# First key products by full-width weights: a re-planned start of an attention and state-space kernel

## The chip, the cores and the metric

The kernel runs on one core of a Trainium2 chip. The metric is the device time of one execution in microseconds (us); smaller is better. A core has five engines with queues of their own: PE (TensorE, matrix products; its weight loads are shown as PEld), DVE (VectorE), ACT (ScalarE), POOL (GpSimd) and SP (SyncE, which here only issues DMA transfers). They wait for one another by semaphores.

## The reference

Two blocks of 2048 positions and 640 channels, whose results are put side by side. A is a state-space layer: a complex recurrence along the positions, run between two products with dense matrices. B is attention with 32 query heads of 20 channels which share one key head and one value head.

```
def _A_ref(x, ...):
    Lam_bar = exp(exp(log_dt) * Lam);  B_bar = ((Lam_bar - 1) / Lam)[:, None] * B
    Bu = einsum("bld,pd->blp", x, B_bar)
    h[t] = Lam_bar * h[t-1] + Bu[t]              # for all 2048 t
    return 2 * real(einsum("blp,dp->bld", h, C)) + x * Dskip

def _B_ref(x, wq, wk, wv, wo):
    q = (x @ wq) as 32 heads of 20;  k = x @ wk;  v = x @ wv
    p = softmax(q @ k^T * 20 ** -0.5)            # for each head, 2048 x 2048
    return (p @ v, heads side by side) @ wo
return concatenate([a, b], axis=-1)              # bfloat16
```

## The kernel before

**Tiles.** Scores are made transposed: 128 keys by 512 queries of one head are one tile, a matrix product of 32 rows, and there are 2048 tiles. ACT takes the exponential of two or three tiles that lie side by side in PSUM with one instruction (L1481, 1024 or 1536 columns). The other tiles (a share of 0.29) go to DVE, which turns scores into bfloat16 bits by integer arithmetic (L863, from PSUM into BIG); each such tile is copied three times with integer offsets, by POOL in pairs (L1796) or by DVE. PE multiplies all of them with the values (PR with VP, BIG with VS) and adds them up in one bank. The state-space layer and the projections ride along between score products as background tasks.

**A planned order.** The program is not written in the order in which it runs. `Build` submits operations with an engine, a duration, dependencies and a priority; `Schedule.run` plays them through against its own durations, always starting the ready operation with the lowest priority number on a free engine; `planned` does this for 32 seeds (L550) and keeps the plan whose replays end first. The order of each engine's queue and every wait come from that plan. Constants such as the landing times `LANDS` and `XB`, the duration given to an operation, and its `prio` therefore move the order, also long after the place where they stand.

**The start.** Ahead of the first exponential lies this:

- SP loads blocks 0 and 1 of x (512 positions each) as they are, then a part of the query weights, and then issues three transposing loads (L711) for block 2, the first three column chunks of block 3 and its last two (`XB`). ACT's queue loads the key weights into `wkr` (L706).
- PE turns blocks 0 and 1 by products with the identity (`turn`, four products for each of 5 chunks of 128 channels); the turned chunk is copied out of PSUM by DVE (L1121, "d") or ACT (L1124, "a"), as `TURNED` says for each block.
- `kv(tb)` makes the keys of block tb. Each key column is wanted four times, on the four strips of 32 rows. Blocks below `QUAD_KEYS` get this by four products with 32 columns of `wkr`, which run side by side (`four`); the others by one product with 128 columns of `wks`, a copy of `wkr` with every column group four times (L1035, on POOL). Block 3 is done in two halves of 256 columns in the order of `KEY_STEPS`, since its last two chunks land last.
- DVE finds the largest magnitude of the keys (L1152, L1178), `KT` is evicted by DVE or ACT as `KEYS` says (L1158 or L1161), a bound is made from the maximum (`bound`, L1180) and added to the first query row with four products (L1280), DVE evicts it as QT (L1286), and the first scores follow.
- At the same time the scalars of the state-space layer (`ssm_scalars`) run through PE, DVE and ACT, up to tables of sines (`fr` on DVE and POOL, L2135 on ACT).
- While PE has nothing else to do, `warm_source` gives it products with zeros (MB from PR) to keep it busy; later ones with VZ.

**What the edit touches**: `warm_source` (L912 to L927), the loads of L1031 to L1038, the constants of L1070 to L1074, the products and the reduction in `kv` (L1137 to L1155) and `KEY_STEPS` (L1247). In this kernel those that are read as lines of the profile are L726 (products made by `mm`), L1146 (key products with `wks`), L1263 (first query products), L1035 (the copy to `wks`) and L1202 (value products).

Of the kernel before, what the change touches and what calls it, by code (L numbers as in the profile page):

```python
# [11 lines left out]
ACT = mybir.ActivationFunctionType  # L12
ALU = mybir.AluOpType
AX = mybir.AxisListType
FP32 = mybir.dt.float32
# [441 lines left out]
S, D, NC, H, DH = 2048, 640, 5, 32, 20  # L457
# [8 lines left out]
class Build:  # L466
# [445 lines left out]
    def warm_source(self):  # L912

        if self.pv_first or self.s.t > 40000.0:
            return None
        p = self
        if self.started:
            if self.s.recent(3000.0) > self.WARM:
                return None
            fns = self.four(self.pvbank, [p.VZ[:]] * 4, p.KT[:, 0:512], True, True)  # L920
            return Op("pe", fns, self.mmt(512), prio=3.5, mode="C", load=512.0, reads=["VZ", "KT0"], writes=[self.pvbank.key],
                      deps=[self.c_op["VZ"], self.kt_op[0]])
        return Op("pe", [self.mm(self.pvbank.ap, p.PR[:, 0, 0:128], p.PR[:, 0, :], True, True)], 440.0 if self.s.t < 5000.0 else 250.0, prio=9,
                  load=512.0, deps=[self.zero_op], reads=["PR0"], writes=[self.pvbank.key], hook=self.warm_last)

    WARM = 4500.0
    V_AT, V_BY = (-97.5, -95.5), (22, 34)  # L927


# [89 lines left out]
    def loads(self):  # L1019
        p = self  # L1020
# [14 lines left out]
        self.wks_op = self.pool(lambda e: e.tensor_copy(spread, again), 800, deps=[self.wk_op], reads=["wkr"], writes=["wks"],  # L1035
                                prio=self.WKP, port=True)
        self.vec_op.append(vec[3]("sp"))
        self.wqa_op = L(wqd[:, :, 0:80], wqv[:, :, 0:80], 200000, "wqa", strided=True, writes=["wqa"], prio=0)  # L1038
        for tb, lo, hi, at in self.XB:
# [3 lines left out]
            for c in range(lo, hi):  # L1043
                self.xb_op[tb, c] = o
        self.wv_op = L(p.wvr[:], p.wv.rearrange("(c p) n -> p c n", p=128), 228000, "wv", strided=True,
                       writes=["wvr"])
# [5 lines left out]
                                prio=0.9, port=True)  # L1052
        for o, t in zip(self.vec_op + self.xn_op + [self.wk_op, self.wqa_op, self.wv_op, self.wq_op], self.LANDS):
            o.lands = t
# [4 lines left out]
                       writes=[f"xaT{tb}_{c}_{eo}" for tb in range(2) for c in range(NC)], gate=self.bound_made) for eo in range(2)]  # L1059
# [50 lines left out]
    def kv_steps(self):  # L1110
        p = self
# [19 lines left out]
        def kv(tb):  # L1131
            yield lambda: all((tb, c) in self.xb_op for c in range(NC)) and (tb < self.PLAIN or self.s.done([self.xb_op[tb, 0]])) \
                and any(x in self.early for x in self.free_banks)
            bank = self.take(self.early, self.KEY_BANKS)
            prev = None
            parts = 1 if tb < 3 else 2
            n = 512 // parts  # L1137
            steps = [(x, c) for x in range(parts) for c in range(NC)] if tb < 3 else self.KEY_STEPS
            for x, c in steps:
                at = 512 * tb + n * x  # L1140
                if tb < self.QUAD_KEYS:
                    prev = self.pe(self.four(bank, [p.wkr[:, c, :]] * 4, p.xbT[:, c, at:at + 512], c == 0, c == NC - 1), self.mmt(512),
                                   mode="C", prio=self.KP[tb], deps=[self.xb_op[tb, c], self.wk_op] + bank.last, prev=prev,
                                   reads=[f"xbT{tb}_{c}", "wkr"], writes=[bank.key])
                else:
                    prev = self.pe([lambda e, x=x, c=c, at=at: e.matmul(bank.cols(n * x, n * x + n), lhsT=p.wks[:, 128 * c:128 * c + 128],  # L1146
                                                                        rhs=p.xbT[:, c, at:at + n], start=c == 0, stop=c == NC - 1,
                                                                        skip_group_check=True)],
                                   self.mmt(n), prio=self.KP[tb], deps=[self.xb_op[tb, c], self.wks_op] + bank.last, prev=prev,
                                   mode="F", load=float(n), reads=[f"xbT{tb}_{c}", "wks"], writes=[bank.key])  # L1150
                if c == NC - 1:
                    red = self.dve(lambda e, src=bank.cols(n * x, n * x + n), to=p.mab[:, tb + x:tb + x + 1]: e.tensor_reduce(  # L1152
                        out=to, in_=src, axis=AX.X, op=ALU.max, apply_absolute_value=True), 115 + 1.05 * n, deps=[prev], reads=[bank.key],
                        writes=[f"mab{tb + x}"], prio=0.31 if x == parts - 1 else 0.315)
                    self.red_op[tb + x] = red  # L1155
            dst, src = p.KT[:, 512 * tb:512 * tb + 512], bank.ap
            if self.KEYS[tb] == "a":
                kt = self.act(lambda e: e.activation(dst, src, ACT.Identity, bias=p.lift[:, 2:3], scale=ALPHA * UNIT), 600,  # L1158
                              deps=[red, self.lift_op], reads=[bank.key, "lift"], writes=[f"KT{tb}"], prio=0.34)
            else:  # L1160
                kt = self.dve(self.ts(dst, src, ALPHA * UNIT, p.lift[:, 2:3], ALU.mult, ALU.add), 640,  # L1161
                              deps=[red, self.lift_op], reads=[bank.key, "lift"], writes=[f"KT{tb}"], prio=0.44)
            self.kt_op[tb] = kt
            yield lambda: kt.start is not None
            bank.last = [kt]
            self.give(bank)
            if tb < 2:
                yield lambda: any(x in self.early for x in self.free_banks)
                yield from self.v_task(tb, self.take(self.early, self.KEY_BANKS))
            else:  # L1170
                self.tasks.append((self.V_AT[tb - 2], 0, lambda: self.started, lambda bank: self.v_task(tb, bank)))
                self.tasks.sort(key=lambda t: t[0])
# [1404 lines left out]
```

## Time and profile before

| | before |
|---|---|
| runs, us | 708.70, 708.71, 708.75 |
| median, us | 708.71 |
| the profiled execution, device time, us | 708.9 |
| its span, first to last instruction, us | 707.2 |
| granted TensorE clock, mean | 1.000 |
| first exponential starts, us | 19.38 |
| last exponential ends, us | 698.83 |
| DMA traffic, mean over the span | 49 GB/s |

Busy time is the time in which at least one instruction of an engine ran. A row of the costliest groups reads: line, engine, operation, output from input, shapes, count, then busy us, mean ns of one, and the engine's idle time just before them with what ended it. A row of a timeline reads: start, length, engine, line, operation; neighbours of one kind are merged, and the bracket is idle time before the first. A row of the chain of waits in order of time reads: start, length, engine, line. The span's first 20 us are shown in more detail by the views quoted below than by the page, whose slices are 17.7 us long.

### The profile page before, as it was taken

The page shows a single profiled execution, that of the slowest core. Times are in us where ns is not written, and L with a number is a line of the kernel's source. Part 1 is how long each engine was busy: PE and PEld are TensorE (multiplying, and loading weights), DVE is VectorE, ACT ScalarE, POOL GpSimd, SP SyncE. Part 2 cuts the span into 40 slices and gives each one's busy share as a digit, 9 for nine tenths or more (in the row PEclk, how much of TensorE's full clock was granted, in tenths as well). Part 3 has the DMA queues.
Part 4 walks back from the last instruction along what each step waited for, and adds up shares of the span by engine and source line. Part 5 has one row for each costly group of instructions (what it writes and reads, how often), then busy time and mean ns, then how long its engine had stood idle before and what let it go on. Part 6 is the DMA issues. An engine that isn't in the chain of part 4 may idle for free.

```text
span 707.2 us, 26738 instructions
## 1 busy us (share of the span) xinstructions
PE 689.4 (97%) x11235; PEld 247.7 (35%) x11235; DVE 621.2 (88%) x1193; ACT 690.3 (98%) x698; POOL 462.4 (65%) x784
## 2 busy tenths in 40 slices
PE   8999999999999999999999999999999999999997
PEld 4322233443333533334333333333333333343323
DVE  7899999999899788878889998899999997978794
ACT  6999999999999999999999999999999999999996
POOL 4266574046787566955857847766767768778880
PEclk9999999999999999999999999999999999999999
DMA  9577741021120010103001010121000011100001
GB/s 224 145 173 164 160 112 52 25 48 31 26 50 13 18 26 27 38 20 66 18 18 29 19 28 26 43 57 19 13 14 20 13 22 35 39 20 20 21 15 40
DMA packets 77590, 34.44 MB, mean 49 GB/s; under 512 B 58351, under 2 KB 77471, under 8 KB 77471
## 3 DMA queue, kind: packets, MB, share of 16 engines
q1 hardware_dynamic: 76506, 32.44, 19.0%
q8 instruction: 90, 1.47, 0.9%
q10 hardware_dynamic: 964, 0.29, 0.2%
q14 instruction: 30, 0.24, 0.1%
HBM read 11.53 MB, written 9.75 MB: 30 GB/s over the span
## 4 chain that ended last, share of the span: by engine, by line
ACT 56%; PE 36%; DVE 4%; SPq 1%; DMA 1%; issue 1%; POOL 1%; DVEq 0%; POOLq 0%
ACT PR L1481 56%; PE MB L726 13%; PE MB L796 10%; PE SC L726 8%; PE MB L806 4%; DVE BIG L863 2%; SPq L711 1%; PE SC L796 1%; DMA BIG<-in_B_x_dram 1%; POOL BIG L1796 1%; PE SC L722 0%; DVE prod L858 0%; DVE BIG L1303 0%; SPq L707 0%; DVE stg L2048 0%
## 5 line engine op out<-in xcount | busy, mean ns | idle before, releaser
L1481 ACT ACTIVATE PR<-SC 128x1024 bf16<-128x1024 f32 (+1 forms) x677 | 676.7, 1190 | 4.3 <-PE SC L726 3.0
L1796 POOL INT64_ADD BIG<-BIG x748 | 449.3, 617 | 216.3 <-DVE BIG L863 102.7
L863 DVE TENSOR_SCALAR BIG<-SC 128x512 int16<-128x512 f32 x532 | 358.1, 686 | 62.7 <-PE SC L726 55.3
L726 PE MATMUL SC<-QT,KT 32*128 32x512 bf16 x2011 | 264.8, 384 | 7.6 <-ACT PR L1481 3.2
L726 PE MATMUL MB<-BIG,VS 128*32 128x512 bf16 x2276 | 256.8, 384 | 0.0
L726 PE MATMUL MB<-PR,VP 128*32 128x512 bf16 x1479 | 216.8, 384 | 0.0
L726 PEld LDWEIGHTS SC<-QT,KT 32*128 32x128 bf16 x2011 | 68.0, 90 | 177.3 <-ACT PR L1481 105.6
L726 PEld LDWEIGHTS MB<-BIG,VS 128*32 128x32 bf16 x2276 | 61.3, 94 | 65.5 <-issue 42.0
L726 PEld LDWEIGHTS MB<-PR,VP 128*32 128x32 bf16 x1479 | 52.6, 94 | 44.5 <-issue 31.8
L796 PE MATMUL MB<-CT,W 128*32 128x320 bf16 (+2 forms) x1008 | 53.2, 301 | 0.2
L863 DVE TENSOR_SCALAR BIG<-BIG 128x1024 int16<-128x1024 int16 (+1 forms) x110 | 42.0, 417 | 4.4 <-PE MB L726 4.2
L796 PE MATMUL MB<-CA,W 128*32 128x512 bf16 (+1 forms) x640 | 36.4, 302 | 0.9 <-issue 0.8
L806 PE MATMUL MB<-xaT,BT 32*128 32x256 bf16 x176 | 34.0, 272 | 1.3 <-ACT PR L1481 1.1
L796 PE MATMUL MB<-xaT,BA 128*32 128x256 bf16 x800 | 32.6, 275 | 0.0
L806 PE MATMUL MB<-diagD,xaT 32*128 32x128 bf16 x320 | 31.3, 217 | 0.0
L796 PEld LDWEIGHTS MB<-CT,W 128*32 128x32 bf16 x1008 | 23.2, 96 | 16.6 <-issue 7.4
L806 PEld LDWEIGHTS MB<-diagD,xaT 32*128 32x128 bf16 x320 | 17.7, 92 | 28.4 <-ACT PR L1481 17.3
L796 PE MATMUL MB<-xaT,BT 128*32 128x256 bf16 x624 | 26.3, 274 | 0.0
L858 DVE TENSOR_TENSOR prod<-MB,tab 128x1024 bf16<-128x1024 f32 x20 | 24.4, 1218 | 1.7 <-PE SC L726 1.0
L863 DVE TENSOR_SCALAR BIG<-MB 128x512 int16<-128x512 f32 x37 | 25.2, 680 | 0.2 <-PE MB L726 0.2
L2048 DVE CAST stg<-MB 128x512 bf16<-128x512 f32 x35 | 23.8, 679 | 1.2 <-PE MB L796 0.8
L796 PE MATMUL MB<-WO,OP 128*32 128x128 bf16 (+1 forms) x480 | 23.3, 301 | 0.2
(170 smaller groups left out, 467.9 us busy)
## 6 DMA issues: line engine op xcount, KB each, us to landing
out_dram<-stg SPq DMA_DIRECT2D x31, 128.0 KB, 1.9
qd<-BIG SPq DMA_DIRECT2D x20, 128.0 KB, 2.4
QT<-qd SPq DMA_DIRECT2D x28, 80.0 KB
OP<-pvsb SPq DMA_DIRECT2D x105, 20.0 KB
rdP<-recs SPq DMA_DIRECT2D x105, 20.0 KB
lbd<-BA SPq DMA_DIRECT2D x5, 320.0 KB, 2.8
CT<-in_B_x_dram SPq DMA_DIRECT2D x2, 640.0 KB, 5.3
BA<-in_A_B_re_dram SPq DMA_DIRECT2D x1, 800.0 KB, 7.0
```

The lines of the kernel that those rows point to most:

```text
L711: fns = [lambda e, o=o, i=i: e.dma_start_transpose(o, i) for o, i in pairs]
L726: return lambda e: e.matmul(out, lhsT=lhsT, rhs=rhs, start=start, stop=stop, **kw)
L796: x = e.matmul(out[32 * j:32 * j + 32], lhsT=lhsT[:, 32 * j:32 * j + 32], rhs=rhs, start=start, stop=r.end is tag, tile_position=(0, 32 * ...
L806: return lambda e: e.matmul(out, lhsT=lhsT[at], rhs=rhs[at], start=False, stop=r.end is tag, tile_position=(32 * row, 0), skip_group_check ...
L858: return lambda e: e.tensor_tensor(out, a, b, op)
L863: return lambda e: e.tensor_scalar(out, a, s1, s2, op0=op0, op1=op1)
L1481: ex = self.act(lambda e: e.activation(dst, t[:, 0:512 * n], ACT.Exp, scale=1.0 / UNIT), 0.8333 * 512 * n + 64, table="exp", deps=[op], re ...
L1796: op.fns.append(lambda e: e.int64_add(words(dst), words(src), add))
L2048: ev = self.dve(lambda e: e.tensor_copy(st, bank.ap), 645, deps=[prev], reads=[bank.key], writes=[key], prio=self.EV, gate=(lambda: last.e ...
```

## The change

The keys of block 0 are made like those of the other blocks, with the four-fold weights (`QUAD_KEYS` 0); the copy that makes these is on ACT (`WKE` "a") instead of POOL. Blocks 0 and 1 have their turned chunks copied by ACT, DVE, ACT, DVE, ACT instead of DVE first; the keys of block 0 are evicted by ACT and those of block 1 by DVE. In block 3 the first three chunks are done 512 columns wide and only the last two in halves. Filler products planned before 4 us read the zeros as fp32, 256 columns wide. `FRP`, the priority of the table's DVE steps, is 0.34, and the key weights are expected on the chip at 6500 ns of the plan instead of 7000.

```diff
@@ warm_source
-        return Op("pe", [self.mm(self.pvbank.ap, p.PR[:, 0, 0:128], p.PR[:, 0, :], True, True)], 440.0 if self.s.t < 5000.0 else 250.0, prio=9,
+        wide = p.PR[:, 0, :].bitcast(FP32)
+        long = self.s.t < self.LONG_TO
+        zeros, dur = (wide, 850.0 if self.s.t < 5000.0 else 440.0) if long else (p.PR[:, 0, :], 440.0 if self.s.t < 5000.0 else 250.0)
+        return Op("pe", [self.mm(self.pvbank.cols(0, zeros.shape[-1]), zeros[:, 0:128], zeros, True, True)], dur, prio=9,
                   load=512.0, deps=[self.zero_op], reads=["PR0"], writes=[self.pvbank.key], hook=self.warm_last)
-    WARM = 4500.0
+    WARM, LONG_TO = 4500.0, 4000.0
@@ loads
-        self.wks_op = self.pool(lambda e: e.tensor_copy(spread, again), 800, deps=[self.wk_op], reads=["wkr"], writes=["wks"],
-                                prio=self.WKP, port=True)
+        if self.WKE == "a":
+            self.wks_op = self.act(lambda e: e.activation(spread, again, ACT.Copy), 650, deps=[self.wk_op], reads=["wkr"], writes=["wks"],
+                                   prio=0.34)
...
@@ constants
-    PLAIN, KP, QR, FRP, SINP, SKIP_P, KEY_BANKS = 2, (1.04, 1.04, 1.06, 1.08), 1.05, 0.36, 0.32, 1.03, "2543016"
-    WKP, QUAD_KEYS = 0.9, 1
-    TURNED, KEYS = ("dadad", "dadad"), "daaa"
+    PLAIN, KP, QR, FRP, SINP, SKIP_P, KEY_BANKS = 2, (1.04, 1.04, 1.06, 1.08), 1.05, 0.34, 0.32, 1.03, "2543016"
+    WKP, QUAD_KEYS, WKE = 0.9, 0, "a"
+    TURNED, KEYS = ("adada", "adada"), "adaa"
-    LANDS = (2250.0, 2400.0, 2750.0, 8200.0, 5600.0, 7900.0, 7000.0, 8450.0, 14600.0, 17000.0)
+    LANDS = (2250.0, 2400.0, 2750.0, 8200.0, 5600.0, 7900.0, 6500.0, 8450.0, 14600.0, 17000.0)
@@ kv
-            parts = 1 if tb < 3 else 2
-            n = 512 // parts
-            steps = [(x, c) for x in range(parts) for c in range(NC)] if tb < 3 else self.KEY_STEPS
-            for x, c in steps:
+            steps = [(0, c, 512) for c in range(NC)] if tb < 3 else self.KEY_STEPS
+            for x, c, n in steps:
...
-                        writes=[f"mab{tb + x}"], prio=0.31 if x == parts - 1 else 0.315)
+                        writes=[f"mab{tb + x}"], prio=0.31 if tb < 3 or x else 0.315)
@@
-    KEY_STEPS = ((0, 0), (0, 1), (0, 2), (1, 0), (1, 1), (1, 2), (0, 3), (0, 4), (1, 3), (1, 4))
+    KEY_STEPS = ((0, 0, 512), (0, 1, 512), (0, 2, 512), (0, 3, 256), (0, 4, 256), (1, 3, 256), (1, 4, 256))
```

More of the change, by code (lines that the diff above doesn't have):

```diff
@@ L1034, in loads @@
         spread = p.wks[:].rearrange("p (c j n) -> p c j n", c=NC, j=4)
-        self.wks_op = self.pool(lambda e: e.tensor_copy(spread, again), 800, deps=[self.wk_op], reads=["wkr"], writes=["wks"],
-                                prio=self.WKP, port=True)
+        if self.WKE == "a":
+            self.wks_op = self.act(lambda e: e.activation(spread, again, ACT.Copy), 650, deps=[self.wk_op], reads=["wkr"], writes=["wks"],
+                                   prio=0.34)
+        elif self.WKE == "d":
+            self.wks_op = self.dve(lambda e: e.tensor_copy(spread, again), 400, deps=[self.wk_op], reads=["wkr"], writes=["wks"],
+                                   prio=0.34, port=True)
+        else:
+            self.wks_op = self.pool(lambda e: e.tensor_copy(spread, again), 800, deps=[self.wk_op], reads=["wkr"], writes=["wks"],
+                                    prio=self.WKP, port=True)
         self.vec_op.append(vec[3]("sp"))
@@ L1145, in kv @@
                 else:
-                    prev = self.pe([lambda e, x=x, c=c, at=at: e.matmul(bank.cols(n * x, n * x + n), lhsT=p.wks[:, 128 * c:128 * c + 128],
+                    prev = self.pe([lambda e, x=x, c=c, n=n, at=at: e.matmul(bank.cols(n * x, n * x + n), lhsT=p.wks[:, 128 * c:128 * c + 128],
                                                                         rhs=p.xbT[:, c, at:at + n], start=c == 0, stop=c == NC - 1,
```

## The prediction

> **What bounds the kernel now.** I read the page first: engine shares, then the chain that ended last, then the costliest groups.
>
> ```profile
> span 707.2 us, 26738 instructions
> PE 689.4 (97%) x11235; PEld 247.7 (35%) x11235; DVE 621.2 (88%) x1193; ACT 690.3 (98%) x698; POOL 462.4 (65%) x784
> ACT 56%; PE 36%; DVE 4%; SPq 1%; DMA 1%; issue 1%; POOL 1%; DVEq 0%; POOLq 0%
> L1481 ACT ACTIVATE PR<-SC 128x1024 bf16<-128x1024 f32 (+1 forms) x677 | 676.7, 1190 | 4.3 <-PE SC L726 3.0
> ```
>
> ACT is busy 98% of the span, nearly all of it in the 677 exponentials of L1481. So the span is three pieces: what comes before the first exponential, the stream of exponentials, and a tail. Next I read the chain of waits in order of time for the first 22 us, which tells what the first piece is made of.
>
> ```profile
> 3.20 5.29 SPq L711
> 8.54 1.46 SPq L711
> 10.04 5.55 DMA BIG<-in_B_x_dram
> 15.64 0.62 PE SC L1146 x4
> 16.29 0.77 DVE mab L1152 x2
> 17.08 0.17 DVE mab L1178
> 17.27 0.30 DVE M L862
> 17.61 0.40 PE MB L726 x4
> ```
>
> Columns are start, us, what. SP issues three transposing loads of x back to back from 3.20; the last lands at 15.59. Only then do the last four key products run, then two reductions, the bound, four small products, the eviction of QT, and the first scores. The start hangs on that landing. Third, the timelines of ACT and POOL.
>
> ```profile
> 6.40 1.08 ACT L1124 ACTIVATE BIG<-SC 128x512 bf16<-128x512 f32 x2 [0.18 <-PE SC L726]
> 8.73 1.08 ACT L1124 ACTIVATE BIG<-SC 128x512 bf16<-128x512 f32 x2 [1.24 <-PE SC L726]
> ...
> 17.08 0.69 ACT L1158 ACTIVATE KT<-SC,lift 128x512 bf16<-128x512 f32 x1 [1.53 <-DVE mab L1152]
> 6.88 0.72 POOL L1035 COPY wks<-wkr 128x640 bf16<-128x640 bf16 x1
> 15.64 0.61 PE L1146 MATMUL SC<-BIG,wks 128*128 128x256 bf16 x4 [1.66 <-DMA BIG<-in_B_x_dram]
> ```
>
> Brackets give the idle time just before: ACT waits 1.24 and 1.53 us in this stage, PE 1.66 us for the landing. Last, the stream: counts by shape, and two runs in which nothing was late.
>
> ```profile
> L1481 ACT ACTIVATE PR<-SC 128x1024 bf16<-128x1024 f32 x552 | 519.5, 1106 | 3.9 <-PE SC L726 2.9 <-PE MB L726 0.6
> L1481 ACT ACTIVATE PR<-SC 128x1536 bf16<-128x1536 f32 x125 | 178.4, 1564 | 0.4 <-PE MB L726 0.2 <-PE SC L726 0.2
> 113.27 22.96 ACT L1481 ACTIVATE PR<-SC 128x1536 bf16<-128x1536 f32 x17
> 134.56 1.67 ACT L1481 ACTIVATE PR<-SC 128x1536 bf16<-128x1536 f32 x1
> 281.50 11.10 ACT L1481 ACTIVATE PR<-SC 128x1024 bf16<-128x1024 f32 x12
> 291.45 1.16 ACT L1481 ACTIVATE PR<-SC 128x1024 bf16<-128x1024 f32 x1
> ```
>
> Instructions overlap, so the price is the step from start to start: (134.56 - 113.27)/16 = 1.331 us for 1536 columns, (291.45 - 281.50)/11 = 0.9045 us for 1024. The difference, 0.426 us, buys 512 columns; what is left, 0.9045 - 0.852 = 0.052 us, is the fixed part of one instruction. The first exponential starts at 19.38 and the last ends at 698.83, so the stream takes 679.45 us. Its steps make 552 x 0.9045 + 125 x 1.331 = 665.6, and the last one ends 0.3 after its step (1.63 against 1.33). The rest, 13.5 us, is **loss**: exponentials that came late, mostly by too little to show as idle. The tail is 707.2 - 698.83 = 8.4 us.
>
> **The change, part by part.** All edits lie ahead of the first exponential, but the kernel's order is planned as a whole, so the rest moves too; I read that from the order of instructions of both kernels.
>
> *ACT before the stream.* Turned copies on ACT rise from 4 to 6, two more at 1.08/2 = 0.54 us. The copy that spreads the key weights comes to ACT behind the first turned copy. No row shows ACT copying 640 columns from SBUF; the nearest are 0.54 (512 columns) and 1.04 (the 1024-column table), so 0.5 to 1.0, and I take 0.68 (0.54 x 640/512). Of the three key evictions one stays swapped (block 0 to ACT, block 1 to VectorE), so their number is the same. Added: 1.08 + 0.68 = 1.8 us. It lies in ACT's idle 1.24 + 1.53 = 2.8 us. The weights were on the chip in time: POOL copied them at 6.88 with no idle time before it, and ACT reaches its copy at about 6.94. Queued behind this copy are five turned copies, the table, the first QT eviction and the key evictions, which all move by what the idle time does not swallow ahead of them; the last one, at 17.08, waits for VectorE anyway. POOL sheds 0.72 us and VectorE two casts of 0.64, both off the path. VectorE's five table steps now all stand ahead of its first cast, which moves from 6.18 to about 7.0 (three more at 0.29); the product of that chunk waits for the weights until 7.6 anyway.
>
> *PE before the landing.* Block 0's 20 quarter-width key products become 5 full ones. A full one steps by 0.215 us (the five query products of L1263 take 1.24 with the last one's 0.38), four quarter ones run side by side in 0.40 with theirs, so the array's time is the same and I put 0. But they now wait for the weight copy, 6.40 + 0.54 + 0.68 = 7.6, instead of starting at 6.96, and two of them stand in PE's queue ahead of the second batch of transposes. That batch moves from 8.07 to about 8.2, or 8.5 with the fillers' delay below. From there the steps add up: batch and vector product 1.3, eight key products 1.7, five query products 1.1, eight more key products 1.7, and 0.2 of latency. PE is done at 14.2 to 14.5 where it now is at 14.0. The landing at 15.59 hides it, with 1.1 us to spare; if the landing came 1.6 us earlier, this would set the start.
>
> *Last block's keys.* Six products of 256 columns become three of 512: the same columns, ahead of the landing, 0. The four behind it stay (0.62 us), as do the reductions.
>
> *Fillers.* Ahead of the first transposes stand 8 fillers instead of 12, 5 of them fp32 of 256 columns. A bf16 filler takes 0.42 us there (weight loads for it step from 2.09 to 2.51); an fp32 one is not in the trace, so I bound it by half a filler (0.21) and two (0.84). Three stand ahead of the small vector product at 3.50: 1.26 + 3 x 0.84 = 3.8 at worst, a delay of 0.3 us for the chain of scalars, the table load and ACT's first turned copy. I take that, 0.3. With it ACT's shift is 2.1, still under 2.8. [...]
>
> *SP's queue* keeps its order up to the bound's DMA: the same four loads, then the three transposes. So the landing stays, and the first piece is 19.38, plus 0; bounds -0.2 and +0.5.
>
> *The stream.* It has 562 of 1024, 118 of 1536 and one of 512 columns instead of 552 and 125. The tiles are the same, 2 x 562 + 3 x 118 + 1 = 1479 = 2 x 552 + 3 x 125, so VectorE's share is too. Four instructions more: 4 x 0.052 = **+0.2 us**. [...]
>
> The loss of 13.5 us is redrawn, since hardly an instruction of the stream keeps its place. I split it by stretches between ACT's visible gaps. From 58.63 to 336.44, 195 and 73 exponentials, it is 277.8 - 273.5 = 4.3 us, 1.55 per 100 us; from 628.88 to 675.00, 46 and 2, it is 46.1 - 44.3 = 1.85 us, 4.0 per 100; the mean is 2.0. Over 679 us the mild rate would make 10.5, a quarter of the stream at the bad rate 16.9. I take 13.5 again: VectorE does 12 pair copies fewer and POOL 11 more, which speaks for a little less, but nothing gives a size.
>
> *The tail.* From the last exponential on, PE's, ACT's and VectorE's steps come in the same order, one group of 16 in another bank: 8.4, plus 0, bounds -0.3 and +0.3.
>
> Sum: 19.4 + (665.8 + 0.3 + 13.5) + 8.4 = 707.4 us of span, 0.2 more than now. The profiled execution took 708.9 us over its span of 707.2, and the median of the runs is 708.71, 1.5 above the span: **708.9 us**. I call anything within 0.2%, 1.4 us, no change; that is about what a measurement of this kernel can tell from none.
>
> **Rivals.**
> 1. *The new order loses less* (0.18). Everywhere the mild rate: loss 10.5, so 3.0 off and 0.2 on: 705.9. For it: VectorE, at 88%, is relieved by about 5 us (12 x 0.42). Against: the mild rate held for one long stretch, never for the whole.
> 2. *The new order loses more* (0.27), the case on the other side. A score fill on PE comes late because VectorE has not yet emptied the bank; the waits list has PE's weight loads for scores waiting 42.9 us in 100 places for that. If this makes a quarter more of the stream, 170 us, run at 4.0 per 100 instead of 2.0, it costs 3.4 us: 712.3. It decides from a loss of 14.7 on. For it: such stretches exist, and the present order is one draw with no reason to be the worse one. Against: VectorE has less to do.
> 3. *ACT's copy of the weights becomes the start* (0.03). If the weights land late or the copies on ACT run longer than the rows, all that is queued behind shifts past 2.8 us; 1 us beyond gives 709.9.
> 4. *The start gets shorter* (0.03): were the landing not the bound, the shorter key path could bring at most PE's wait, 1.66 us: 707.3. Against it: the bracket on L1146 names the DMA.
>
> The forecast, start kept and loss within 1.4 of now, has 0.49.
>
> **How the numbers follow.** Faster: rival 1 and half of rival 4, 0.20. Same: forecast, rival 3, half of 4, 0.53. Slower: rival 2, 0.27. The forecast's own range is 707.5 to 710.1. For 8 in 10 I reach into both redraws, leaving a tenth outside at each end: 706.5 to 711.6.
>
> **What would show it.** First exponential within 0.5 us of 19.38, still behind the landing near 15.6; the copy of the weights on ACT near 7 us and 0.5 to 1.0 long; a tail of 8.4; 681 exponentials at the same steps. The whole difference should then be the loss. I am wrong if the start moves by over 0.5 us or if the loss leaves 10.5 to 16.9.

## The result: 0.17% faster, with an earlier first exponential

| | median, us | all runs, us | runs | ratio to before | 95% interval |
|---|---|---|---|---|---|
| before | 709.23 | 708.34 to 710.38 | 20 | | |
| after | 708.25 | 707.24 to 708.89 | 20 | 0.9983 | 0.9976 to 0.999 |
| before, a second time | 709.37 | 708.38 to 710.81 | 11 | 1.0001 | 0.9993 to 1.001 |
| after, a second time | 708.86 | 708.3 to 709.13 | 11 | 0.9989 | 0.9981 to 0.9998 |

The last two rows are experiments told below, against runs of before on their own chip (709.13, 35 runs). The three runs of before that stand ahead of the prediction had a median of 708.71; 709.23 is that of the 20 beside after's. The forecast was 708.9, 0.2 us slower than those three; by the ratio the change took 1.2 us off, 0.7 to 1.7 by its interval; the medians differ by 0.98. The time lies in the range given, but the sign was wrong.

First the page of after: the span, the share of ACT, the chain that ended last, and the costliest group.

```profile
span 707.2 us, 26749 instructions
PE 692.6 (98%) x11246; PEld 248.8 (35%) x11248; DVE 618.2 (87%) x1181; ACT 691.6 (98%) x705; POOL 466.5 (66%) x794
ACT 56%; PE 42%; issue 0%; DVE 0%
L1489 ACT ACTIVATE PR<-SC 128x1024 bf16<-128x1024 f32 (+1 forms) x681 | 676.7, 1199 | 5.0 <-PE SC L726 4.2
```

The span is before's to the tenth, because the execution that was profiled is the slowest of the 20 of after (708.89); the page alone would say that nothing happened. What did change is the third line: the chain of before had 1% of SP's queue and 1% of DMA in it, the chain of after has none. The chain of waits of after in order of time (start, length, what) shows where these went:

```profile
1.25 5.86 PE MB L726 x14
7.11 1.12 PE SC L726 x20
...
13.39 2.18 PE SC L1154 x12
...
15.59 0.77 DVE mab L1160 x2
...
16.91 0.40 PE MB L726 x4
...
18.36 0.34 PE SC L726 x2
...
18.72 2.86 ACT PR L1489 x3
```

Before ran through SP's issue of the transposing loads and 5.55 us of waiting for the third to land. After runs through PE from 1.25 to 15.57: fillers, transposes, key products. It never waits for that load. Splitting both pairs of profiled executions into start, stream and tail as the prediction does, with the loss being what the steps from exponential to exponential take over their nominal 0.9045 and 1.331 us:

| profiled execution | time | span | first exponential | stream | its loss | tail |
|---|---|---|---|---|---|---|
| before | 708.9 | 707.2 | 19.38 | 679.45 | 13.55 | 8.33 |
| after | 708.89 | 707.2 | 18.72 | 680.26 | 14.14 | 8.17 |
| before, second | 709.46 | 707.7 | 19.56 | 679.92 | 14.00 | 8.25 |
| after, second | 708.42 | 706.7 | 18.61 | 679.90 | 13.77 | 8.17 |

The start is shorter in both pairs, by 0.66 and 0.95 us. The stream differs by +0.81 and -0.02, where two executions of one kernel differ by 0.47 (before) and 0.36 (after), so two pairs show no difference of the stream that holds. What both pairs share is the earlier start. So the question was what had shortened a start that was said to hang on a landing which the edit does not touch.

### The profile page after: what moved, and what is told of

It reads as the page before. It is cut to its first block, busy times and chain, and to the rows that moved or that the text cites. A ratio compares the mean times of both kernels' runs of the same rounds, so it can differ in the third digit from the quotient of the medians.

```text
span 707.2 us, 26749 instructions
## 1 busy us (share of the span) xinstructions
PE 692.6 (98%) x11246; PEld 248.8 (35%) x11248; DVE 618.2 (87%) x1181; ACT 691.6 (98%) x705; POOL 466.5 (66%) x794
## 4 chain that ended last, share of the span: by engine, by line
ACT 56%; PE 42%; issue 0%; DVE 0%
ACT PR L1489 56%; PE MB L726 17%; PE MB L796 10%; PE SC L726 10%; PE MB L806 4%; PE SC L1154 1%; PE SC L722 0%; PE MB L1271 0%; DVE mab L1160 0%; DVE BIG L863 0%; PE SC L1210 0%; ACT PR L2051 0%; DVE pvsb L858 0%; DVE M L862 0%; DVE PR L964 0%
## 5 line engine op out<-in xcount | busy, mean ns | idle before, releaser
L1804 POOL INT64_ADD BIG<-BIG x759 | 454.2, 615 | 214.8 <-DVE BIG L863 75.0
L726 PE MATMUL MB<-PR,VP 128*32 128x512 bf16 x1479 | 205.0, 385 | 0.0
L726 PEld LDWEIGHTS MB<-BIG,VS 128*32 128x32 bf16 x2276 | 59.3, 94 | 63.5 <-issue 42.1
L726 PEld LDWEIGHTS MB<-PR,VP 128*32 128x32 bf16 x1479 | 48.9, 94 | 49.7 <-issue 38.5
L863 DVE TENSOR_SCALAR BIG<-BIG 128x1024 int16<-128x1024 int16 (+1 forms) x100 | 39.8, 424 | 2.6 <-PE MB L726 2.3
L806 PE MATMUL MB<-xaT,BT 32*128 32x256 bf16 x160 | 30.9, 272 | 0.7 <-ACT PR L1489 0.7
```

The source lines that it names most:

```text
L726: return lambda e: e.matmul(out, lhsT=lhsT, rhs=rhs, start=start, stop=stop, **kw)
L806: return lambda e: e.matmul(out, lhsT=lhsT[at], rhs=rhs[at], start=False, stop=r.end is tag, tile_position=(32 * row, 0), skip_group_check ...
L863: return lambda e: e.tensor_scalar(out, a, s1, s2, op0=op0, op1=op1)
L1804: op.fns.append(lambda e: e.int64_add(words(dst), words(src), add))
```

## The experiments

### What was suspected

The trace records when each of the 16 parts of a transposing load lands, and each fetch of instructions. In before, 15 parts of the third load had landed by 14.21 and the last came at 15.59. A 16 KB instruction fetch ran from 13.32 to 14.49. In after the load is complete at 14.71, and the first such fetch comes at 18.74. The DMA view of 13.2 to 14.6 us lists queues with packets, MB and share. In before:

```profile
q1 hardware_dynamic: 873, 0.14, 101.4%
q8 instruction: 1, 0.02, 5.2%
```

and in after, where q8 is missing:

```profile
q1 hardware_dynamic: 1264, 0.25, 113.4%
```

Theory T1: the fetch holds up the load. PE's instruction count ahead of the start decides where the fetch falls, and the change lowered it (5 products for 20 in block 0, 7 for 10 in block 3, and 8 fillers for 12, though the trace records each of the five fp32 ones as two products, so 13 for 12). In before's trace 90 of the 120 fetches are of 16 KB, and in its second run the first four of these come after 185, 437, 730 and 978 of PE's records, 248 to 293 apart.

### Both kernels again

Before, unchanged:

> The kernel before, unchanged, for a second profile and a comparison with itself. Theory 1 (a straggler): in the first profile 15 of the 16 parts of the last transposing load had landed at 14.21 us and the sixteenth at 15.59, while a 16 KB instruction fetch ran at 13.32 to 14.49 us. If the fetch does it, it comes at the same place of the program each time: landing near 15.6 and first exponential near 19.4 again. Rival (chance): the late part is an accident of that one execution, and the landing lies near 14.2 and the start near 18.0 here. Ratio 1.000 within 0.1% either way.

After, unchanged:

> The changed kernel, unchanged, for a second profile. Theory 1: no fetch near 13 us, landing near 14.7 us, and PE's queue, not the landing, sets the first exponential; with the full clock granted earlier than the 6.50 us of the first profile the start is earlier than 18.72, down to about 18.0; stream 680.3 and tail 8.2 as in the first profile; ratio 0.998 to 0.999. Rival (the stream): the start is as in the kernel before, and the stream is shorter than 679.5 us in most executions.

The times are in the first table. Chain of waits, before's second run:

```profile
10.08 5.69 DMA BIG<-in_B_x_dram
...
15.82 0.62 PE SC L1146 x4
```

and after's second run:

```profile
13.28 2.18 PE SC L1154 x12
...
18.61 2.86 ACT PR L1489 x3
```

Both starts repeat: fetch at 13.54, last part at 15.77, 1.3 us behind the other fifteen; in after no fetch until 19.14, load complete at 14.39. The late part is no accident of one execution.

### The fetch moved by PE's instruction count

Four kernels leave the planned order as it is and change what PE has to run ahead of the start: three issue some of its products in pieces, one takes other fillers.

Before with each filler in four:

```diff
-        return Op("pe", [self.mm(self.pvbank.ap, p.PR[:, 0, 0:128], p.PR[:, 0, :], True, True)], 440.0 if self.s.t < 5000.0 else 250.0, prio=9,
+        fns = [self.mm(self.pvbank.cols(128 * i, 128 * i + 128), p.PR[:, 0, 0:128], p.PR[:, 0, 128 * i:128 * i + 128], True, True) for i in range(4)]
+        return Op("pe", fns, 440.0 if self.s.t < 5000.0 else 250.0, prio=9,
```

> The kernel before with its own plan, each filler product of 512 columns issued as four of 128: the same time on PE, but some 36 products and as many weight loads more ahead of the first transposes, so that PE's instruction fetches fall at other moments. Theory 1: no 16 KB fetch between 12.5 and 15 us, the last load lands near 14.2 us, the first exponential starts near 18.0 instead of 19.4, and the time is 1.0 to 1.4 us shorter (ratio 0.998). Rival (chance, or the transfer itself is slow): landing and start as in the kernel before, ratio 1.000.

Before with each filler in two (the same lines with 256 for 128 in the columns written and read, and `range(2)`; the weights stay 128 columns wide):

> Before's order, each filler ahead of the first scores issued as two of 256 columns: 24 PE instructions and weight loads more before the start instead of the 72 of the split in four. T1: the fetch moves ahead of 13.5 us by 1 to 3 us; if it is over by 12.5 the load lands whole at 14.3 to 14.6 and the first exponential starts at 18.1 to 18.7; if it still overlaps 13 to 14.4 the load's last part lands at 15.4 or later and the start stays at 19.3 to 19.6. R1: start 19.3 to 19.6 whatever the fetch does. For the stream, theory T2 (its loss moves with the places at which PE's instructions are fetched, since PE stands still where a dense run of small products meets a fetch): loss anywhere from 13.5 to 16.5, with the difference to before sitting in a few single late exponentials of 0.5 to 1 us, each behind a pause of PE that nothing on the chip explains. Rival R2 (the loss is a matter of the planned order alone): 13.5 to 14.0 as in both runs of before.

After with each key product in two:

```diff
-                    prev = self.pe([lambda e, x=x, c=c, n=n, at=at: e.matmul(bank.cols(n * x, n * x + n), lhsT=p.wks[:, 128 * c:128 * c + 128],
-                                                                        rhs=p.xbT[:, c, at:at + n], start=c == 0, stop=c == NC - 1,
-                                                                        skip_group_check=True)],
+                    h = n // 2
+                    prev = self.pe([lambda e, x=x, c=c, n=n, at=at, i=i, h=h: e.matmul(bank.cols(n * x + i * h, n * x + i * h + h),
+                                                                        lhsT=p.wks[:, 128 * c:128 * c + 128],
+                                                                        rhs=p.xbT[:, c, at + i * h:at + i * h + h], start=c == 0, stop=c == NC - 1,
+                                                                        skip_group_check=True) for i in range(2)],
```

> The change's order, each key product issued as two halves of its columns: some 22 products and 22 weight loads more, all between 8.6 and 15.3 us, the fillers untouched, so the clock should come as in the change (6.2 to 6.5 us). Theory T1 (a 16 KB instruction fetch that runs while a transposing load of x is in flight holds that load up by about 1 us; in the change the fetch falls behind the loads): the fetch moves from 18.5 to 19.1 ahead to 12 to 15, the third load's last part lands at 15.3 to 16.0 instead of 14.4 to 14.7, and the first exponential starts 3.8 behind it, at 19.1 to 19.8; time 0.4 to 1.0 us above the change's (709.0 to 709.6). Rival R1 (the loads land earlier in the change for another reason): landing 14.3 to 14.8, first exponential 18.6 to 19.0 wherever the fetch is. If the fetch does not come between 11 and 15, the run decides nothing.

Before with the change's fp32 fillers and nothing else of it (8 products for 12, recorded as 13):

> Before with the change's fp32 fillers alone; all other instructions keep their order. PE has 4 products and 4 weight loads fewer ahead of the start (8 if an fp32 product counts once), so the fetch should slip behind 13.5 us by some 0.3 to 1.5 us. T1: if it starts behind 14.4 the third load lands whole at 14.3 to 14.7 and the first exponential comes at 18.1 to 18.9, time 0.5 to 1.2 below before; if it still starts ahead of 14.2, the last part lands at 15.3 to 16.2 and start and time stay before's (19.2 to 19.8; 708.9 to 709.5). R5: the time falls by 0.5 or more whatever the landing does.

All kernels of the study, in the order of their first fetch. The loads' columns give the landing of the last part (us from the start of the span); where one part came over 1 us behind the rest, the other fifteen stand first.

| kernel | 16 KB fetch | load 1 | load 2 | load 3 | first exp. |
|---|---|---|---|---|---|
| before, fillers in four | 10.06 to 11.02 | **11.91** | 13.46 | 14.42 | 18.58 |
| before, fillers in two | 11.59 to 12.77 | 11.22 | **14.30** | **15.33** | 19.12 |
| before, in four, short store | 12.12 to 13.29 | 11.35 | **14.25** | **15.45** | 19.61 |
| before | 13.32 to 14.49 | 11.24 | 13.08 | 14.21, **15.59** | 19.38 |
| after, key products in two | 13.42 to 14.61 | 11.28 | 13.12 | 14.34, **15.64** | 19.48 |
| before, second | 13.54 to 14.73 | 11.25 | 13.23 | 14.46, **15.77** | 19.56 |
| before, fp32 fillers | 14.05 to 15.31 | 11.29 | 13.31 | 14.62 | 19.07 |
| after, fillers in four | from 17.26 | 11.32 | 13.21 | 14.44 | 23.90 |
| after | from 18.74 | 11.24 | 13.36 | 14.71 | 18.72 |
| after, single bf16, short store | from 18.91 | 11.33 | 13.24 | 14.48 | 19.03 |
| after, bf16 in pairs | from 19.12 | 11.28 | 13.20 | 14.34 | 18.82 |
| after, second | from 19.14 | 11.27 | 13.17 | 14.39 | 18.61 |
| after, before's fillers | from 19.26 | 11.31 | 13.26 | 14.50 | 18.32 |
| after, single bf16 fillers | from 19.94 | 11.32 | 13.15 | 14.31 | 18.13 |

The late load follows the fetch from row to row: at 10 us it is the first, at 12 the second (and the third behind it), at 13.4 one part of the third, and with no fetch among them all three land within 0.4 us of the same times. How much of a load is held up differs: one part of 16 in three rows, 11 in one, and all of them for the second load of before with fillers in two. There the traffic of all of the core's DMA nearly stops from about 12.1 to 13.5 us; GB/s from 11 to 14 us in 40 slices:

```profile
GB/s 123 215 276 283 297 294 280 515 266 266 280 273 260 203 62 31 10 0 7 7 17 10 7 7 17 7 7 10 10 10 7 10 10 62 290 290 287 294 287 160
```

The sharpest row is after with its key products in two: the fetch comes back to 13.42, and with it the whole picture of before, in its DMA view of 13.2 to 14.6 us

```profile
q1 hardware_dynamic: 969, 0.16, 89.5%
q8 instruction: 1, 0.02, 5.3%
```

and in its chain of waits:

```profile
10.05 5.59 DMA BIG<-in_B_x_dram
...
15.69 0.64 PE SC L1155 x8
...
19.48 1.94 ACT PR L1491 x2
```

Its median is 709.34 us (12 runs), 1.0007 of before (0.9993 to 1.0021): the gain of the change is gone, though everything else of it is there. T1's numbers for it were 15.3 to 16.0, 19.1 to 19.8, and 709.0 to 709.6; its rival's 14.3 to 14.8 and 18.6 to 19.0. T1 stands, as far as the load goes: the fetch holds it up, in a way that the traces don't show.

The count of instructions is only a part of what places the fetch. Before with fillers in four and the same with a short store have the same PE instructions, and their fetches start at 10.06 and 12.12; in the second PE came to the same place later, with the full clock at 8.92 instead of 6.96. With fp32 fillers PE's transposes begin 1.5 us later than in before (7.29 against 5.75), and the fetch 0.5 to 0.7 later. In before it starts when 185 to 189 of PE's records have begun; after has as many at 15.7 to 15.9, behind the landing, but its fetch starts some 3 us later still, for which no reason was found.

Three of these runs missed a part of what was expected. With fillers in four the load landed whole, at 14.42, but the first exponential came at 18.58 instead of near 18.0, and the time did not fall (710.79; see below). With halves a fetch that ends at 12.8 was to leave the load whole at 14.3 to 14.6; it held up the second load instead, and the third landed behind it at 15.33. With fp32 fillers the fetch started at 14.05, where T1 wanted a late part, and the load landed whole: a fetch that began 0.9 us ahead of the landing of the fifteen parts (three rows) held up the last, one that began 0.57 ahead of the landing did not. There the start gained only 0.31 to 0.49, because PE is late; its chain of waits:

```profile
1.25 6.20 PE MB L726 x14
...
13.78 2.19 PE SC L1149 x15
```

The key products end at 15.96, behind the landing of 14.62. Its median is 708.76, 0.9991 of before (0.9981 to 1.0001); since the landing moved too, this run does not tell the fillers' share from the fetch's. The halves in before took 709.65, 1.0008 (1.0 to 1.0017).

### What the fillers do

After with its plan, but the five fp32 fillers issued as single bf16 products, which take half the time (0.427 us for 0.85):

```diff
-        zeros, dur = (wide, 850.0 if self.s.t < 5000.0 else 440.0) if long else (p.PR[:, 0, :], 440.0 if self.s.t < 5000.0 else 250.0)
+        zeros, dur = p.PR[:, 0, :], (850.0 if self.s.t < 5000.0 else 440.0) if long else (440.0 if self.s.t < 5000.0 else 250.0)
```

> The changed kernel's own plan, but the five fp32 fillers are bf16 of 512 columns again (the plan still counts the long duration). They took two passes of 0.427 us each, so PE is 5 x 0.43 = 2.1 us less busy ahead of the first transposes. Theory 1 with PE as the bound: PE reaches the last four key products before the landing, so the start moves from 18.72 to the landing plus 3.7 us, about 18.4, and the time falls by 0.2 to 0.7 us against the changed kernel. Rival (fillers are hidden or help the clock): start within 0.1 of the changed kernel's or later, time the same or longer.

After with all fillers in four pieces:

```diff
-        return Op("pe", [self.mm(self.pvbank.cols(0, zeros.shape[-1]), zeros[:, 0:128], zeros, True, True)], dur, prio=9,
+        q = zeros.shape[-1] // 4
+        fns = [self.mm(self.pvbank.cols(q * i, q * i + q), zeros[:, 0:128], zeros[:, q * i:q * i + q], True, True) for i in range(4)]
+        return Op("pe", fns, dur, prio=9,
```

> After's order, each filler ahead of the first scores issued as four quarters (4 x 64 columns of fp32, 4 x 128 of bf16): the same columns, some 50 PE instructions more before the start. Theory T1 (the start of before is late because a 16 KB instruction fetch runs while the third transposing load lands and holds up one of its 16 parts; the change got rid of it only by having fewer PE instructions ahead): the fetch, at 18.5 to 19.1 us in the change, moves ahead to 12 to 14.5, the last part of the load lands at 15.4 to 16.0 instead of 14.4 to 14.7, and the first exponential starts at 19.2 to 19.8 instead of 18.6 to 18.7; time 0.6 to 1.2 us above the change's. Rival R1 (the load lands earlier in the change for another reason, such as the new order of copies or the free queue): landing stays at 14.3 to 14.8 wherever the fetch runs, first exponential 18.5 to 18.9.

After with two bf16 products for each fp32 one:

```diff
-        return Op("pe", [self.mm(self.pvbank.cols(0, zeros.shape[-1]), zeros[:, 0:128], zeros, True, True)], dur, prio=9,
+        fns = [self.mm(self.pvbank.ap, p.PR[:, 0, 0:128], p.PR[:, 0, :], True, True) for i in range(2 if long else 1)]
+        return Op("pe", fns, dur, prio=9,
```

> The change's order, each of the five fp32 fillers issued as two bf16 ones of 512 columns, which take the same 0.85 us. [...] Rival R4 (the type or the smaller number of instructions matters): full clock at 6.9 or later in the profiled run, or a spread of over 2.5 us and a median of 709.3 or more, as with single bf16 fillers.

After with before's fillers, five and seven (the same, but one product instead of two for the third of the five):

> The change's order with before's own row of fillers: five bf16 ahead of the small vector product, seven behind it. Theory T5 (once the fetch is out of the way the landing at 14.4 bounds the start, unless PE is later, and PE is later in the change only because its fp32 fillers delay the first transposes by 1.2 us): vector product at 3.5, transposes from 5.8, full clock at 4.9 to 6.0, the landing at 14.3 to 14.7 and the first exponential 3.8 behind it, 18.1 to 18.4; of the 0.3 to 0.5 us gained on the change up to 0.3 is lost again at 31 us, where the bound's way through memory is then late: time 708.0 to 708.8. Rival R5 (fp32 fillers are what brings the gain of the change): 709.0 to 709.6, as with the single bf16 fillers.

| | median, us | all runs | ratio to before | 95% interval |
|---|---|---|---|---|
| single bf16 | 709.29 | 708.51 to 710.19 | 1.0003 | 0.9994 to 1.0012 |
| in four pieces | 715.79 | 715.3 to 716.02 | 1.0097 | 1.0084 to 1.011 |
| bf16 in pairs | 708.06 | 707.5 to 708.72 | 0.9983 | 0.9974 to 0.9993 |
| before's fillers | 708.24 | 707.6 to 710.01 | 0.9987 | 0.9976 to 0.9997 |

*Pieces.* The run was to move the fetch ahead to 12 to 14.5 and moved it to 17.26 only, so it says nothing on T1. It shows that PE bounds the start. PE's timeline:

```profile
1.25 5.38 PE L726 MATMUL MB<-PR 128*128 128x64 f32 x24 [1.25 <-DVE PR L966]
...
6.69 4.96 PE L726 MATMUL MB<-PR 128*128 128x64 f32 x28
```

An fp32 product is recorded as two passes. For 256 columns each pass steps by 0.427 us, for 64 columns by 0.213 instead of the 0.107 that a quarter would be. The first transposes came at 11.44 instead of 6.95, and the first exponential 5.2 us later.

*Pairs.* In time, type fp32 is worth nothing by itself: the ratio is the change's own, 0.9983. The first exponential came at 18.82, 0.10 and 0.21 behind the change's two. The full clock came at 7.08, and 6.9 or later was a sign of R4; its other sign, a median of 709.3 or more with a wide spread, did not come: 708.06, with a spread of 1.22.

*Before's fillers.* They end at 6.64, 0.47 us sooner than the change's, and the start follows with 0.40. T5 wanted transposes from 5.8, as in before; the clock came at 6.36 instead of 4.90, so the fillers ran longer at the slow step of 0.427 us. The chain of waits runs through PE:

```profile
1.26 5.38 PE MB L726 x13
...
12.92 2.25 PE SC L1155 x12
...
18.32 2.89 ACT PR L1490 x3
```

But PE and the landing meet here, as the row of the last four key products shows:

```profile
14.54 0.61 PE L1155 MATMUL SC<-BIG,wks 128*128 128x256 bf16 x4
```

That is 0.04 us behind the landing of 14.50, as in before (15.64 behind 15.59), and the first exponential comes 3.82 behind it, as T5 said.

With the fetch gone, before's fillers do as well as the new ones, so R5 falls.

*Single bf16.* The start was the earliest of all, 18.13, now 3.8 behind the landing, as Theory 1 had it; but the time was to fall by 0.2 to 0.7 us against the change and rose by 0.4 (708.86 on the same chip), as the rival had it, and the median is not below before's. Two things may take the start back; that they make up the median is argued, not shown. PE idles ahead of the transposes, and how fast these go then differs between executions. The PE timeline of this kernel:

```profile
5.80 1.56 PE L726 MATMUL SC<-ident,CT 128*128 128x128 bf16 x20 [0.57 <-DMA CT<-in_B_x_dram]
```

and that of the kernel with the same PE instructions that is told next:

```profile
5.72 2.31 PE L726 MATMUL SC<-ident,CT 128*128 128x128 bf16 x20 [0.50 <-DMA CT<-in_B_x_dram]
```

The trace's record of the clock has full speed from 6.40 in the first and from 9.25 in the second, whose first exponential came at 19.03. Over all profiles the full clock came between 4.90 and 9.25 us, and at 13.14 with the pieces. The two here are 2.85 us apart with the same PE instructions; what sets the moment was not shown. The second thing is the loss, 14.74 against 13.77 in after's second run: 0.24 of that is in the first 50 us, where an exponential comes 0.31 late at 31 us, which the next experiment is about, and 0.50 at 340 us, behind a pause of PE of 0.99 where after's second run has 0.53.

### A start that is earlier than what follows it

Both the fillers in four (before's plan) and the single bf16 fillers (after's) lost some of their early start at once. Chain of waits of the former:

```profile
16.45 12.03 DMA mrep<-mab
...
28.49 2.91 DMA mcol<-mrep
...
31.43 0.33 DVE Mm L858
```

and ACT's timeline there:

```profile
34.25 2.11 ACT L1482 ACTIVATE PR<-SC 128x1024 bf16<-128x1024 f32 x2 [0.84 <-PE SC L726]
```

The bound goes out to memory and comes back spread over the partitions. It lands at about the same time however early the start is (store landed at 27.54 in before's second run from an issue at 17.44, at 28.48 here from 16.45), and VectorE waits 1.1 us for it. The median of this kernel is 710.79, 1.0021 of before (1.0006 to 1.0037): the start gained 0.8 to 1.0, the stream's loss rose from 13.55 and 14.00 to 16.44. Of the rise of some 2.6, 0.98 is at 34 us, and 0.98 in one exponential at 339.76 us behind a pause of PE of 0.89 us for which nothing on the chip is named, 0.6 us after a fetch had ended. T2, by which the stream's loss follows the places of the fetches, fits that one; the fillers in two, with a loss of 14.09, speak neither for nor against it.

In two kernels the store was cut from 640 numbers to 160, the rest being repeats, with the load reading overlapping windows (the tensor in memory is made shorter to match):

```diff
-            many = bass.AP(tensor=p.mab, offset=5, ap=[[8, DH], [0, H], [1, 1]])
+            many = bass.AP(tensor=p.mab, offset=5, ap=[[8, DH], [0, 8], [1, 1]])
...
-            back = self.load(p.mcol[:], p.mrep.rearrange("(c p) -> p c", p=128), 2560, "mi", strided=True, deps=[out], reads=["mrep"],
+            back = self.load(p.mcol[:], bass.AP(tensor=p.mrep.tensor, offset=0, ap=[[1, 128], [8, NC]]), 2560, "mi", strided=True, deps=[out], reads=["mrep"],
```

Before's plan with fillers in four:

> The split in four of before's fillers again, and the bound's store to memory written as 160 numbers instead of 640 (each fourth part of the store was a repeat of the same numbers; the load reads overlapping windows). Theory T3 (the 0.98 us that the earlier start lost again at 34 us is the wait for the bound's way through memory, 11 us long from its issue at 16.45, which stood in the chain of waits there): the store lands by 22 to 25 instead of 28.48, the exponential at 34 us comes with less than 0.2 lost, the loss of the first 50 us of the stream falls from 2.52 to 1.3 to 1.6, the total loss from 16.4 to 15.2 to 15.6, time 1 us below the split alone (709.8). Rival R3 (the store waits for the transfers ahead of it in the same rings, not for its own pieces): it lands at 27 to 28.5 as before and nothing changes.

After's plan with single bf16 fillers:

> The change's order with bf16 fillers, whose first exponential started at 18.13, and the bound's store as 160 numbers instead of 640. T3: the exponential that came 0.31 late at 31 us comes on time, loss of the first 50 us 0.5 to 0.65 instead of 0.88; with the start at 18.1 the span should be 706.2 to 707.0, a median of 707.9 to 708.9. T2: the pause of PE at 338.7 us (0.99 against the change's 0.53) stays, since the PE instructions are the same. R3: loss of the first 50 us 0.85 to 0.95.

Both became slower: 711.99 (1.0045 of before, 1.0031 to 1.0059) and 711.97 (1.005, 1.0034 to 1.0066). The store landed 0.9 and 1.4 us sooner, at 27.56 and 26.25. But in before's plan its length is not what it waits for, as R3 said: issued at 17.48 the short one landed at 27.56, and before's long one, issued at 17.44, at 27.54. In after's order, issued at 16.88, it landed 1.0 us sooner than after's long one, issued at 16.45 (27.24). The load then took 5.7 and 5.3 us where it had taken 2.9 and 2.2. The view of the tile in the first of them:

```profile
  DVE Mm L858: 2.1, 1
...
DMA to landing us min/median/max: 5.7/5.7/5.7
```

T3's remedy failed: the wait grew from 1.1 to 2.1, the loss of the first 50 us of the stream from 2.52 to 4.61, and the whole loss from 16.4 to 18.2. Not all of this is the load. PE stood idle for 1.69 us ahead of 35.67, and the clock then fell to half from 36.23 to 39.64, the only such fall within the stream of any profile here (PE's busy time, granted clock, share of DMA and GB/s from 36 to 40 us):

```profile
36.00:40.00 4.00, 4.00 (x34) 0.57 0.48 153
```

Two exponentials that come 0.84 and 0.35 late in or just behind that stretch are 1.2 of the 4.61. Nor is all of the time the store's doing. The starts were later by 1.03 and 0.90 us than without the short store (19.61 and 19.03), because PE was later, with the full clock at 8.92 and 9.25: its key products end at 16.48 and 15.88. In the second kernel the loss of the first 50 us was 1.7, beyond both T3's 0.5 to 0.65 and R3's 0.85 to 0.95, and the profiled execution is the fastest of six (709.63), so its trace does not show what the median of 711.97 is made of. T2 missed here: the pause at 338.7 us was to stay, since PE's instructions are the same, and it was gone, so more than their count decides on such pauses, and T2 is left open. What holds the store for 10 us was not found; that the load became slow because all its reads hit the same few numbers is only argued.

## Why the prediction was wrong, point by point

- **The failed step** is "SP's queue keeps its order up to the bound's DMA ... So the landing stays, and the first piece is 19.38, plus 0". The queue did keep its order, and the landing moved from 15.59 to 14.71 (15.77 to 14.39). The prediction read the bracket on L1146, which names the DMA, as the load's own length. It was that of fifteen parts plus 1.4 us for one part beside an instruction fetch, and the change moved the fetch behind the loads, since PE has fewer instructions ahead of it and comes to it later (as many of its records as before has at the fetch, 185 to 189, stand in after at 15.7 to 15.9, and with 22 key products more the fetch was back at 13.42).
- **Rival 4, the start gets shorter**, is what happened, though not for its reason; it had 0.03. It rested on the landing not being the bound, and in before it was: the landing itself moved. Its price, 1.66 us, was too large: the start gained 0.66 and 0.95, since PE's own end takes over, as the prediction said it would "if the landing came 1.6 us earlier".
- **PE ahead of the landing** was mis-sized. It was to be ready for the last four key products at 14.2 to 14.5 and came to them at 14.96 (second run 14.84), behind the landings of 14.71 and 14.39, so that it sets the start:

```profile
14.96 0.60 PE L1154 MATMUL SC<-BIG,wks 128*128 128x256 bf16 x4
```

  An fp32 filler takes two passes of 0.427 us, 0.85, close to the upper bound given (0.84); but only the small product's delay was summed (0.3 taken, 0.61 measured, 3.50 to 4.11), not that of all eight fillers, which end 1.20 us later. PE's timeline of after:

```profile
1.25 2.92 PE L726 MATMUL MB<-PR 128*128 128x256 f32 x6 [1.25 <-DVE PR L964]
4.11 0.19 PE L726 MATMUL MB<-ident,vrow 15*128 15x15 bf16 x1
...
6.95 1.28 PE L726 MATMUL SC<-ident,CT 128*128 128x128 bf16 x20
```

  Transposes started at 5.75 before. Of the spare 1.1 us of the prediction some 0.6 would have been left had the landing stayed at 15.59; with the landing at 14.71 there was none. The products of block 0, put at 0, cost none: from the first transpose to the end of the key products PE takes 8.6 us, and before took 8.2 up to its wait (5.75 to 13.98) and 0.6 behind it.
- **ACT's copy of the weights** was right in length, 0.68 taken, 0.73 here, and late by the fillers' delay, 7.87 instead of near 7; ACT's timeline:

```profile
7.37 0.60 ACT L1134 ACTIVATE BIG<-SC 128x512 bf16<-128x512 f32 x1 [0.56 <-PE SC L726]
7.87 0.73 ACT L1039 ACTIVATE wks<-wkr 128x640 bf16<-128x640 bf16 x1
```

  It is not on the chain, so rival 3 stayed away.
- **The stream** was right: 0.2 for four more instructions and the same loss. The loss of single executions moves by more than the forecast's 0.2, but not between the two orders: six profiles with after's order (after twice, key products in two, bf16 single and in pairs, before's fillers) have a mean loss of 13.8, four with before's order (before twice, fillers in two, fp32 fillers) one of 14.0. The other four (fillers in four in either order, and both short stores) lie higher, 14.5 to 18.2; in all four exponentials near 30 to 36 us came 1 to 1.6 us late. Rivals 1 and 2, which had 0.45 between them, did not come.
- **The tail**, 8.4 plus or minus 0.3, was 8.17 both times.

## What to carry to other kernels

A wait that ends with a DMA is not yet the length of that DMA (here 1.4 of 5.55 us were one part's of 16): look at when its parts land, and at what else moved then. Instruction fetches were such traffic here: 22 products more on PE brought one from 18.74 us back to 13.42, and a landing which that edit doesn't touch went from 14.71 to 15.64. Splitting a few products ahead of the spot told the fetch's part from the load's own length. And once a stage's bound is lifted, look for the next one, which here stood less than a microsecond behind (PE at 14.96, the old landing at 15.59): the sum needs the time of the second bound as carefully as that of the first.

## What the hardware showed that was not expected

- A 16 KB instruction fetch of 1.0 to 1.2 us beside a transposing load delayed it by 0.6 to 1.4 us in six profiles: by one of its 16 parts alone in three, by 11 or all of them in two. How the fetch holds them up was not shown.
- The moment of the full clock differed by 2.85 us between two kernels with the same PE instructions (6.40 and 9.25), and by 1.96 between two others (6.96 and 8.92).
- An fp32 product of 64 columns with its own weight load takes half as long as one of 256, not a quarter (0.213 against 0.427 us a pass).
- A round trip of 2.5 KB in single numbers through memory took 12.2 us in before, 13.7 in after and 15.0 in before with fillers in four, from the issue of the store to the landing of the load, and reading it back from a quarter of the addresses was slower by 2.8 to 3.2 us.
